# Talking-heads attention with a squared-ReLU FFN: fusing the first twenty query tiles instead of twelve

## The chip, the cores and the metric

The kernel runs on one core of a Trainium2 chip. The metric is the device time of one execution in microseconds (us). Three runs of the kernel before gave 600.27, 600.85 and 602.12 us; the median, 600.85 us, stands for it. Times inside the execution are read from one profiled execution and are counted from its first instruction. The engines are named as the profile names them: PE is the matrix engine (PEld its weight loads), DVE the vector engine, ACT the scalar engine, POOL the GpSimd engine, and SP the engine that here only issues DMAs.

## The reference, cut to what matters

For each of 8 batches there are 12 heads, 448 positions and a head size of 64. The scores of the heads are mixed by a 12x12 matrix before the softmax, and the probabilities by another one after it; the result, put back into rows of 768, goes through an FFN with a squared ReLU.

```python
scores = scale * np.matmul(q, k.transpose(0, 1, 3, 2))
scores = np.einsum('bhij,hg->bgij', scores, w_pre)
scores = scores - np.max(scores, axis=-1, keepdims=True)
attn = np.exp(scores)
attn = attn / (np.sum(attn, axis=-1, keepdims=True) + 1e-09)
attn = np.einsum('bhij,hg->bgij', attn, w_post)
x = np.matmul(attn, v)            # then rows (b, i) of 12*64 = 768
h = np.maximum(x @ w_in, 0.0)     # 768 -> 2048
out = h * h @ w_out               # 2048 -> 768
```

## The kernel before, in words

**Tiles and steps.** A query tile is 10 query rows with all 12 heads: 120 partitions by 448 keys. There are 45 of them in a batch (the last has 8 rows), 360 in all, and one pass of the main loop (L465) is one step: the mix of tile i, the unmix of tile i - 4 (`LAG`), and pieces of other work between them. Step i begins on PE with the tile's `m_ps` matmul, so the steps can be counted in the trace.

**The mix (L369)** brings the mixed scores of a tile into PSUM (`m_ps`); ACT takes the exponential and the row sum (L384), DVE the reciprocal (L386), and POOL scales the second mixing matrix by it (`pn`, L388). **The unmix (L392)** multiplies the exponentials with `pn` in four matmuls (`at_ps`, L401) and DVE copies the result out (L403).

**Two ways to the mixed scores.** The plain way: a block of 128 query rows is scored head by head (`score_burst`, L320: 12 matmuls `s_ps` over 64 rows of the array, in two bursts of six), ACT and DVE copy the 12 results into an SBUF block `S` (L342, L344; there are two such blocks, used in turn), and SP's queue gathers from it, tile by tile, 10 rows of 12 heads into `G` (L361: 120 pieces of 896 bytes, 105 KB). One matmul of `G` with the mixing matrix then gives `m_ps` (L381). The fused way, for the first `FUSED` = 12 tiles of batch 0: DVE multiplies the queries by the mixing weights beforehand (`mix_queries`, L176), and six matmuls over 128 rows give `m_ps` straight from queries and keys (L376). It needs no `S`, no copies and no gather. The multiplied queries are kept in the FFN's second weights `w2[0..2]`, which are not loaded yet.

In batch 0 the plain tiles are 12 to 44. Their three blocks begin at rows 120, 240 and 320; the first and the third use the same `S` buffer, the second and the first block of batch 1 the other. `BURSTS` says at the issue of which gather the bursts of the next block are put: those of batch 0's third block come at steps 19 and 22, those of batch 1's first block at steps 29 and 32.

**What sets the order.** PE's and POOL's order is the order of the program text; on the others a scheduler sets it. Gathers are issued up to 10 tiles ahead (`AHEAD`), from step 2 on. Loads from HBM that change the type are issued by POOL at fixed steps, each in front of the step's other work: keys and queries of batch 1 at steps 5, 7, ... 15 (`KQ_AT`), the first half of the FFN's first weights (three pieces of 512 KB) before and during the first steps, the second half at steps 18, 21 and 24 (`W1_AT`), the second weights in eight pieces from step 30 to 51 (`W2_AT`). Transposes of batch 1's keys and queries run at steps 17, 21 and 25 (`TURN`), the product with v of the first 15 tiles at step 21.

FFN units are the filler. Batch 0's first FFN half is done in thirds of the positions: 16 units of six matmuls (`h_ps`, L251) for each third, of which the first eight use the first half of the first weights and the last eight the second half. `EARLY` says from which step a group may be spread over the steps: the first third's units from steps 21 (first eight) and 32 (last eight), the second third's from 38, the last third's from 52. ACT takes the ReLU (L257, two buffers `hr`), POOL the square (L262).

The loads of each step, the mix, the fill, the unmix, the gathers and the bursts follow one another like this:

```python
            if s0:
                mix(s0)
            for w, f in now:
                f()
                owed[0] -= w
            fill(share)
            if s1:
                unmix(s1)
...
            if i + 1 < end:
                fill(share)
```

## Time and profile before

| what | value |
|---|---|
| three runs | 600.27, 600.85, 602.12 us |
| the profiled execution, its own time | 600.99 us |
| its span, first to last instruction | 599.2 us |
| PE busy | 574.3 us (96%) |
| DVE / ACT / POOL busy | 69% / 64% / 54% |
| mean granted PE clock | 0.995 |
| start of step 0, 12, 20, 23, 50, 60 on PE | 15.03, 34.17, 44.14, 50.77, 82.36, 99.44 us |

The busy shares are means over stages with different limits. A matmul's record reaches from its start to a modelled end, so a stretch in which matmuls follow each other slowly can look full; the starts of the steps say more than the shares. The last row of the table is counted from the timeline of PE: the n-th tile's first `m_ps` matmul is the start of step n.

### The profile page before, as it was taken

The numbers are of one execution on the slowest core, as the hardware profiler recorded it, in microseconds if no ns is written. First come the engines' busy times: TensorE is split into PE (matmuls) and PEld (weight loads), VectorE is DVE, ScalarE is ACT, GpSimd is POOL, SyncE is SP. The second block draws the span as 40 slices with busy tenths as digits, with TensorE's granted clock in tenths as the row PEclk, the third lists the DMA queues.
The fourth block names the chain that finished last, engine by engine and source line by source line (L and its number), as shares of the span: only waits on it lengthen the run. The fifth ranks groups of instructions, "written<-read, shape, count | busy, mean of one in ns | idle before, by whom it ended". The sixth has DMA issues, their size and how long they took to land.

```text
span 599.2 us, 17220 instructions
## 1 busy us (share of the span) xinstructions
PE 574.3 (96%) x6011; PEld 372.2 (62%) x6011; DVE 411.7 (69%) x1044; ACT 380.6 (64%) x1105; POOL 326.1 (54%) x708
## 2 busy tenths in 40 slices
PE   4979999899999999999999999999999999999996
PEld 3547777566566666566565665666665666666553
DVE  5668769988767777767777777777867667666011
ACT  3757978676876557864776547775677547762410
POOL 5354897362777227862569316792377325761730
PEclk9999999999999999999999999999999999999999
DMA  9898999698569755795458855697544755431003
GB/s 128 141 199 164 191 197 196 128 172 193 100 101 140 145 100 109 121 156 124 98 94 135 151 111 101 113 143 138 109 79 69 133 119 107 84 50 54 27 27 79
DMA packets 88279, 72.28 MB, mean 121 GB/s; under 512 B 6688, under 2 KB 83200, under 8 KB 88192
## 3 DMA queue, kind: packets, MB, share of 16 engines
q1 hardware_dynamic: 50394, 48.16, 36.6%
q0 software_dynamic: 37216, 22.81, 29.3%
q8 instruction: 47, 0.77, 0.5%
q10 hardware_dynamic: 582, 0.21, 0.2%
q14 instruction: 40, 0.33, 0.1%
HBM read 45.70 MB, written 11.01 MB: 95 GB/s over the span
## 4 chain that ended last, share of the span: by engine, by line
PE 81%; DMA 10%; ACT 3%; issue 2%; DVE 1%; POOL 1%; SPq 1%; ACTq 0%; POOLq 0%; DVEq 0%
PE o_ps L295 24%; PE h_ps L251 22%; PE at_ps L401 10%; PE m_ps L381 10%; DMA G<-S 7%; PE ot_ps L209 6%; PE s_ps L332 4%; PE tr_ps L193 3%; ACT e L384 2%; DMA w<-in_moe_w_in_dram 2%; DMA kst<-in_k_dram 1%; ACT S L342 1%; PE m_ps L376 1%; DVE S L344 1%; PE s_ps L338 1%
## 5 line engine op out<-in xcount | busy, mean ns | idle before, releaser
L403 DVE CAST at<-at_ps 112x480 bf16<-112x480 f32 x360 | 228.5, 650 | 73.3 <-PE at_ps L401 72.8
L384 ACT ACTIVATE e<-m_ps 120x448 bf16<-120x448 f32 x360 | 195.5, 547 | 98.8 <-PE m_ps L381 92.4
L388 POOL TENSOR_SCALAR pn<-post,rc 120x120 bf16<-120x120 bf16 x348 | 129.0, 372 | 207.1 <-DVE rc L386 147.6
L251 PE MATMUL h_ps<-xt,w 128*128 128x448 bf16 (+2 forms) x960 | 169.6, 315 | 1.1 <-ACT hr L257 0.6
L295 PE MATMUL o_ps<-w,h 128*128 128x384 bf16 x768 | 138.7, 326 | 0.3 <-ACT S L342 0.2
L401 PE MATMUL at_ps<-pn,e 120*128 120x120 bf16 (+1 forms) x1440 | 135.1, 216 | 0.7 <-POOL pn L388 0.5
L401 PEld LDWEIGHTS <-e 120*128 120x128 bf16 (+1 forms) x1440 | 103.9, 98 | 45.0 <-issue 1.4
L381 PE MATMUL m_ps<-G,pre 120*120 120x448 bf16 x348 | 124.6, 358 | 2.1 <-ACT S L342 1.0
L251 PEld LDWEIGHTS <-w 128*128 128x128 bf16 x960 | 84.6, 98 | 57.7 <-issue 5.6
L262 POOL TENSOR_TENSOR h<-hr 128x384 bf16<-128x384 f32 (+1 forms) x144 | 106.1, 738 | 19.4 <-ACT hr L257 15.6
L257 ACT ACTIVATE hr<-h_ps 128x448 f32<-128x448 f32 (+2 forms) x160 | 75.4, 473 | 52.7 <-PE h_ps L251 35.9
L295 PEld LDWEIGHTS <-h 128*128 128x128 bf16 x768 | 72.8, 98 | 48.2 <-issue 5.5
L344 DVE CAST S<-s_ps 128x448 bf16<-128x448 f32 x159 | 89.2, 615 | 4.2 <-DMA G<-S 2.3
L386 DVE RECIPROCAL rc<-sm 120x1 f32<-120x1 f32 x360 | 57.2, 159 | 45.2 <-ACT e L384 37.3
L342 ACT CAST S<-s_ps 128x448 bf16<-128x448 f32 x171 | 79.8, 546 | 11.9 <-PE s_ps L332 8.4
L384 ACT ACTIVATION_READ_ACCUMULATOR e<-m_ps 120x1 f32 x360 | 74.1, 206 | 0.0
L304 DVE COPY osb<-o_ps 128x384 f32<-128x384 f32 x54 | 30.1, 557 | 46.8 <-PE o_ps L295 46.6
L381 PEld LDWEIGHTS <-pre 120*120 120x120 bf16 x348 | 46.1, 133 | 20.9 <-issue 14.6
L332 PE MATMUL s_ps<-kT,qT 64*128 64x448 bf16 x288 | 41.5, 355 | 5.8 <-ACT S L342 4.4
L209 PE MATMUL ot_ps<-at,v 112*64 112x150 bf16 x1152 | 42.6, 230 | 0.0
L209 PEld LDWEIGHTS <-v 112*64 112x64 bf16 x1152 | 38.3, 110 | 4.9 <-issue 4.9
L215 ACT CAST xt<-ot_ps 128x450 bf16<-128x450 f32 (+1 forms) x48 | 25.5, 533 | 20.4 <-PE ot_ps L209 19.9
(45 smaller groups left out, 288.2 us busy)
## 6 DMA issues: line engine op xcount, KB each, us to landing
G<-S SPq DMA_DIRECT2D x284, 105.0 KB
qst<-in_q_dram POOLq DMA_DIRECT2D x24, 224.0 KB, 5.7
kst<-in_k_dram POOLq DMA_DIRECT2D x24, 224.0 KB, 5.2
v<-in_v_dram POOLq DMA_DIRECT2D x24, 224.0 KB, 6.9
G<-S SPq DMA_DIRECT2D x70, 52.5 KB
w<-in_moe_w_in_dram POOLq DMA_DIRECT2D x6, 512.0 KB, 10.3
w<-in_moe_w_out_dram POOLq DMA_DIRECT2D x8, 384.0 KB, 7.7
out_dram<-osb SPq DMA_DIRECT2D x8, 336.0 KB
```

What stands on the lines that cost most here:

```text
L209: nc.tensor.matmul(ps[64 * hh:64 * hh + 64, TQ * y:TQ * y + TQ], lhsT=vs[b][0:PR, g, r, :], rhs=at[0:PR, r, g, :], start=(y == 0 and r == ...
L251: nc.tensor.matmul(ps[:, 0:n], lhsT=w1[ft // 8][:, c2, ft % 8 * 128:ft % 8 * 128 + 128], rhs=xts[b][:, c2, n0:n1], start=(c2 == 0), stop=( ...
L257: nc.scalar.activation(out=hr[:, 0:n], in_=ps[:, 0:n], func=ACT.Relu)
L262: eng.tensor_tensor(out=dst[:, x - o:y - o], in0=hr[:, x - n0:y - n0], in1=hr[:, x - n0:y - n0], op=ALU.mult)
L295: nc.tensor.matmul(ps[:, 0:384], lhsT=lhsT, rhs=w2[ft // 4][:, ft % 4, nt * 384:(nt + 1) * 384], start=(ft == 0), stop=(ft == FT - 1))
L342: nc.scalar.copy(out=sb[:, h, :], in_=ps[:, 0:S])
L344: nc.vector.tensor_copy(out=sb[:, h, :], in_=ps[:, 0:S])
L381: nc.tensor.matmul(ps[0:n, 0:S], lhsT=m[0:n, 0:n], rhs=Gs.pop(s)[0:n, :], start=True, stop=True)
L384: nc.scalar.activation(out=e[0:n, 0:S], in_=ps[0:n, 0:S], func=ACT.Exp, scale=SCALE, accum_out=sm[0:n, 0:1])
L388: nc.gpsimd.tensor_scalar(out=pn[0:n, :], in0=(post_gi if fused else post)[0:n, :], scalar1=rc[0:n, 0:1], scalar2=1.0, op0=ALU.mult, op1=A ...
L401: nc.tensor.matmul(ps[:, RG * r:RG * r + RG], lhsT=e[0:n, PR * r:PR * r + P], rhs=pn[0:n, :], start=True, stop=True)
L403: nc.vector.tensor_copy(out=ats[(b, third)][0:PR, :, :, IQ * tl:IQ * tl + IQ], in_=ps[0:PR, 0:R * RG].rearrange("p (r g i) -> p r g i", r= ...
```

## The change

`FUSED` becomes 20: tiles 0 to 19 of batch 0 are fused. The multiplied queries of the first 12 (`SOON`) stay in `w2[0..2]`; those of tiles 12 to 19 go to three other buffers that are not in use yet (`w2[3]`, the second `v` buffer and one of the two `xt` buffers), and their six multiplications are placed at steps 3, 4 and 5. The remaining 25 tiles of batch 0 come from two blocks, at rows 200 and 320, with first tiles 20 and 32; each has an `S` buffer to itself. The bursts of the second block come at steps 4 and 6, those of batch 1's first block, which uses the first block's buffer again, at steps 27 and 30. Keys and queries of batch 1 are loaded one step sooner; the second half of the first weights is loaded at steps 15, 17 and 19, not 18, 21 and 24, and the units that use it may begin at step 28, not 32. The function `fused_part` holds the six matmuls; it is called only by `mix`, so their place in the order is the old one.

```diff
--- before.py
+++ after.py
@@ -22,12 +22,13 @@
 IQ = 10
 NT = 45
 RG = H * IQ
-FUSED = 12
+FUSED = 20
+SOON = 12
 FQ = FUSED * IQ
 NEAR = 4
-STARTS = {0: (FQ, 2 * FQ, S - 128)}
-FIRST = {0: (FUSED, 2 * FUSED, 3 * FUSED)}
-BURSTS = {0: ([5, 8], [5, 8], [3, 6])}
+STARTS = {0: (FQ, S - 128)}
+FIRST = {0: (FUSED, 32)}
+BURSTS = {0: ([4, 8], [5, 8])}
 for _b in range(1, B):
     STARTS[_b], FIRST[_b], BURSTS[_b] = (0, 128, 256, 384), (0, 13, 26, 39), ([5, 8], [5, 8], [6], [0, 3])
 GATHERS_AT = 2
@@ -38,11 +39,11 @@
 AHEAD = 10
 SCALE = 1.0 / 8.0
 TURN = {0: (17, 17, 21, 21, 25, 25), 1: (20, 20, 24, 24, 28, 28), B: (1 + LAG,) * 3 + (16 + LAG,) * 3}
-KQ_AT = {1: (5, 7, 9, 11, 13, 15), 2: (52, 54, 56, 58, 60, 62)}
-W1_AT = (-1, 1, 3, 18, 21, 24)
+KQ_AT = {1: (4, 6, 8, 10, 12, 14), 2: (52, 54, 56, 58, 60, 62)}
+W1_AT = (-1, 1, 3, 15, 17, 19)
 W2_AT = (30, 33, 36, 39, 42, 45, 48, 51)
 V1_AT = (47, 50, 53)
-EARLY = ((21, 0, 0, 2), (32, 0, 2, 4), (38, 1, 0, 4), (52, 2, 0, 4))
+EARLY = ((21, 0, 0, 2), (28, 0, 2, 4), (38, 1, 0, 4), (52, 2, 0, 4))
 FFN2_AT = 60
 MAIN = 3 * 128
 
@@ -166,14 +167,21 @@
 
     qTs, kTs, xts, h2ts, ats = {}, {}, {}, {}, {}
 
-    qmix = [w2[u][:, :, :].rearrange("p c m -> p (c m)")[:, 0:2 * FQ * H].rearrange(
-        "p (y t g i) -> p y t g i", y=2, g=H, i=IQ) for u in range(NPAIR // 2)]
+    late = [w2[3][:, :, :].rearrange("p c m -> p (c m)"), stage_tile("v", 2)[:, :, :, :].rearrange("p h r d -> p (h r d)"),
+            ffnp.tile([P, NPAIR, S], BF16, name="xt", tag="xt", bufs=2)[:, :, :].rearrange("p c s -> p (c s)")]
+
+    def mixed(u, y, t0, t1):
+        if t0 < SOON:
+            buf, x = w2[u][:, :, :].rearrange("p c m -> p (c m)"), SOON * y + t0
+        else:
+            buf, x = late[u], (FUSED - SOON) * y + t0 - SOON
+        return buf[:, RG * x:RG * (x + t1 - t0)]
 
     def mix_queries(u, t0, t1):
 
         for y in range(2):
             qs = qTs[0][:, 2 * u + y, IQ * t0:IQ * t1].rearrange("p (t i) -> p t i", i=IQ)
-            nc.vector.tensor_tensor(out=qmix[u][:, y, t0:t1, :, :],
+            nc.vector.tensor_tensor(out=mixed(u, y, t0, t1).rearrange("p (t g i) -> p t g i", g=H, i=IQ),
                                     in0=qs.unsqueeze(2).to_broadcast([P, t1 - t0, H, IQ]),
                                     in1=wrep[:, 2 * u + y, :, :].unsqueeze(1).to_broadcast([P, t1 - t0, H, IQ]),
                                     op=ALU.mult)
@@ -352,7 +360,7 @@
         g = work.tile([P, S], BF16, name="G", tag="G", bufs=AHEAD + 2)
         x, end = IQ * t, min(IQ * t + IQ, S)
         while x < end:
-            blk = x // P if b else min(x // FQ, 3) - 1
+            blk = max(y for y, q0 in enumerate(STARTS[b]) if q0 <= x)
             n = min(end, STARTS[b][blk] + P) - x
             o, y = H * (x - IQ * t), x - STARTS[b][blk]
             sb = Sb[(b, blk)]
@@ -366,17 +374,29 @@
             x += n
         Gs[s] = g
 
+    parts = {}
+
+    def fused_part(t, u):
+
+        if t not in parts:
+            parts[t] = [0, bank("m_ps")]
+        if parts[t][0] > u:
+            return
+        parts[t][0] = u + 1
+        for p in (2 * u, 2 * u + 1):
+            nc.tensor.matmul(parts[t][1][0:RG, 0:S], rhs=kTs[0][:, p, :], lhsT=mixed(u, p % 2, t, t + 1),
+                             start=(p == 0), stop=(p == NPAIR - 1))
+
     def mix(s):
         n = rows_of(s[1])
         b, t = s
-        ps = bank("m_ps")
         fused = b == 0 and t < FUSED
         if fused:
-            for p in range(NPAIR):
-                nc.tensor.matmul(ps[0:n, 0:S], rhs=kTs[b][:, p, :],
-                                 lhsT=qmix[p // 2][:, p % 2, t, :, :].rearrange("p g i -> p (g i)"),
-                                 start=(p == 0), stop=(p == NPAIR - 1))
+            for u in range(NPAIR // 2):
+                fused_part(t, u)
+            ps = parts[t][1]
         else:
+            ps = bank("m_ps")
             m = pres[max(x for x in pres if x <= t)] if b else pre
             nc.tensor.matmul(ps[0:n, 0:S], lhsT=m[0:n, 0:n], rhs=Gs.pop(s)[0:n, :], start=True, stop=True)
         e = ets[(NT * s[0] + s[1]) % ND]
@@ -428,7 +448,7 @@
         for u in range(NPAIR // 2):
             turn_unit(0, 0, u)
             mix_queries(u, 0, NEAR)
-            mix_queries(u, NEAR, FUSED)
+            mix_queries(u, NEAR, SOON)
             turn_unit(0, 1, u, nc.scalar.copy)
             if u == 1:
                 score_burst(0, 0, [0, 1])
@@ -497,10 +517,12 @@
                         at_step(i + 3, u)
                 if t1 == NT - 1:
                     at_step(i + 3 if b1 else FFN2_AT, (0, lambda b1=b1: filler.extend(ffn_units(b1))))
+            if 2 < i < 6:
+                mix_queries(i - 3, SOON, FUSED)
             if i < 2:
                 score_burst(0, 0, [2 + 2 * i, 3 + 2 * i])
             for _ in range(2 if i >= GATHERS_AT else 0):
-                if ahead[0] > min(max(i + AHEAD, 2 * FUSED - 1), len(steps) - 1):
+                if ahead[0] > min(max(i + AHEAD, FIRST[0][1] - 1), len(steps) - 1):
                     break
                 b2, t2 = steps[ahead[0]]
                 gather((b2, t2))
```

## The prediction

> **What bounds the kernel now.** I read the page's busy shares and its chain first, then PE's timeline step by step, then the waits.

> ```profile
> PE 574.3 (96%) x6011; PEld 372.2 (62%) x6011; DVE 411.7 (69%) x1044; ACT 380.6 (64%) x1105; POOL 326.1 (54%) x708
> PE 81%; DMA 10%; ACT 3%; issue 2%; DVE 1%; POOL 1%; SPq 1%; ACTq 0%; POOLq 0%; DVEq 0%
> ```

> PE is the bound, but a tenth of the chain is DMA: a part of the run is not PE's. All the change's edits lie in steps 0 to 49. From step 50 on the two programs have the same instructions in the same order on every engine, so the question is when step 50 begins (82.36 us before). In PE's timeline:

> ```profile
> 31.26 0.38 PE L401 MATMUL at_ps<-pn,e 120*128 120x120 bf16 x4
> 31.47 1.30 PE L376 MATMUL m_ps<-kT,w 128*120 128x448 bf16 x6
> 32.61 0.38 PE L401 MATMUL at_ps<-pn,e 120*128 120x120 bf16 x4
> 32.82 1.30 PE L376 MATMUL m_ps<-kT,w 128*120 128x448 bf16 x6
> ...
> 38.66 0.35 PE L381 MATMUL m_ps<-G,pre 120*120 120x448 bf16 x1
> 38.97 0.37 PE L401 MATMUL at_ps<-pn,e 120*128 120x120 bf16 x4
> 39.27 0.96 PE L332 MATMUL s_ps<-kT,qT 64*128 64x448 bf16 x5
> 43.71 0.35 PE L332 MATMUL s_ps<-kT,qT 64*128 64x448 bf16 x1 [3.47 <-ACT S L342]
> 44.14 0.53 PE L381 MATMUL m_ps<-G,pre 120*120 120x448 bf16 x1
> ```

> A fused step takes 1.35 us from start to start (32.82 less 31.47), and PE runs through it; a plain step takes 0.40 us. After step 19 PE puts the third block's first burst and stands still. ACT says why:

> ```profile
> 39.61 0.20 ACT L384 ACTIVATION_READ_ACCUMULATOR e<-m_ps 120x1 f32 x1
> 43.12 1.84 ACT L342 CAST S<-s_ps 128x448 bf16<-128x448 f32 x4 [3.31 <-DMA G<-S]
> ```

> The third block's copies go into the `S` buffer that the gathers of tiles 12 to 23 are still reading; ACT waits for the last of these, and PE for the PSUM banks that ACT doesn't empty. The bill continues:

> ```profile
> core 0: us, PE busy (x) PEld busy (x) DVE busy (x) ACT busy (x) POOL busy (x), PEclk, DMA share, GB/s
> 34.17:44.14 9.97, 6.16 (x82) 3.73 (x79) 7.56 (x22) 5.95 (x21) 6.18 (x14) 1.00 1.14 202
> 44.14:50.77 6.63, 6.60 (x105) 5.21 (x105) 4.07 (x12) 4.15 (x12) 1.52 (x4) 0.74 0.94 191
> 50.77:82.36 31.59, 29.93 (x413) 23.75 (x414) 25.98 (x67) 27.81 (x96) 24.53 (x58) 1.00 0.91 178
> 82.36:99.44 17.08, 16.12 (x227) 12.95 (x225) 13.80 (x52) 13.72 (x49) 14.93 (x28) 1.00 1.15 204
> ```

> These are steps 12-19, 20-22, 23-49 and 50-59. Right after the stall the granted clock averages 0.74 (it is 0.5 for 3.4 us), and PE looks busy at half speed.

> **The change, part by part.**

> *Steps 12 to 19* (before 9.97 us). Each becomes a fused step: 8 x 1.35 = 10.8. The 32 transposes of step 17 stay: that step took 1.74 against 0.40, and 1.41 where nothing else hindered it (steps 65 and 69), so about 1.0. Stall and burst of step 19 go: the third block no longer exists, and the two blocks have a buffer each. Sum 11.8: **+1.8 us**. So the stall alone doesn't pay for the fused matmuls; filling it costs a little more than it. ACT needs about 0.75 (0.55 + 0.20) and DVE 0.81 (0.66 + 0.15) a step, under 1.35, so PE sets this pace.

> *Steps 20 to 22* (before 6.63). The second burst goes: step 22 took 1.51, a plain one 0.40, so -1.1. At full clock step 20 takes 0.40 (before 0.72) and step 21 3.25 (before 4.40): 0.40 for the tile, 1.0 for the transposes, 1.7 for `ot_ps` (66.41 to 68.10 later on), 0.16 for `pre_ps`. Sum 4.05: **-2.6 us**, of which 1.5 are the clock's.

> The row shows only that half clock follows the stall. [...]

> *Multiplying queries* (steps 3-5). The rows of this shape in DVE's timeline give 1.87 us for two of 480 and two of 960 elements, so some 0.62 for a 960: six are 3.7 us of DVE. In the new instruction lists the scheduler puts one ahead of each of the last two early groups, and four among the first copies of `S`. DVE idled 0.22 and 0.40 us ahead of those groups; the first `m_ps` needs the last group only for its fifth matmul, 1.4 us after its first. The reciprocals of tiles 1 to 3 come up to 1 us later, with 4 steps of 1.35 us before PE asks. Between 0 and 0.9 (two multiplications fully exposed less what idled); I take **+0.15**, near the covered end, since every row around it has slack.

> *Steps 23 to 49* (before 31.59). PE has the same work in both programs: 27 mixes and unmixes, the same 29 FFN units, the same bursts of batch 1, only at other steps (eight units now run in steps 26 and 27). Priced back to back by the timeline's own rows (six `h_ps` 0.39, a tile 0.40, `s_ps` 0.095 each, 48 `ot_ps` 1.75, 32 transposes 0.65 in the stream), before needed 26.75 and lost 4.84. Of that 1.9 recurs whatever the order (transposes 0.36, bursts 0.3 each, small gaps 0.3). The other 2.9 are pockets: step 29 lost 1.13 (a burst whose copies met the ReLUs on ACT), step 32 0.71, step 33 0.42 (it waits for the first weights), steps 48-49 0.60 (POOL late), step 28 0.38. After: no wait for the first weights if they land in time, the bursts at steps 27 and 30 carry two units fewer around them in sum, one FFN unit fewer falls into steps 38-49; against that stands the bunch of eight units at 26-27, which POOL squares at some 0.42 us each, about as fast as PE makes them. Ends: -2.9 (all pockets go) to +1.0 (bunch and weights cost more than what goes). I take half of the pockets, **-1.4**, since two of five have a named reason to go.

> *Second half of the first weights.* The old landing and the new need:

> ```profile
> 53.41 9.94 DMA w<-in_moe_w_in_dram
> ```

> That wait was on the chain: PE stood at step 33. Now the last piece is issued behind step 18's `pn`, at about 46, and the DMAs of this queue took 7.8 to 11.5 us from issue to landing between 24 and 54: so 53.8 to 57.5. PE reaches step 29, the first user, at 34.17 + 0.15 + 11.8 + 4.05 + (23 to 28: 7.6 to 8.0) = about 57.8 to 58.2. Cost nothing, with little to spare; what a late landing costs is a rival below. Nothing is exchanged on POOL but the order: three issues of 0.75 us move from steps 18-24 to 15-19, where POOL has 1 us free per step. The gathers shrink by eight; tiles 20-31 are issued from step 2 on as tiles 12-23 were, landing by 43, ahead of step 20 at 46.

> *From step 50*: the same order, nothing to gain; loads and gathers are issued by steps and move along. PE waits about 3 us at steps 72-74 for batch 2's last queries and keys, which land at 111.9 and 114.4 behind a full queue; -0.5 to +0.7.

> Sum: 0.15 + 1.8 - 2.6 - 1.4 = **-2.0 us**. The profiled execution took 600.99 us, 0.02% off the median of 600.85; against the median this is **598.8 us**.

> **The rivals.**

> *The pockets stay.* PE's work is net +7 us, and the stall returns as small waits on ACT and POOL in steps 23-49: the -1.4 becomes 0 to +0.7, the sum -0.6 to +0.1, near **600.5**. For: POOL and ACT are 78% and 88% busy there. Against: ACT and DVE lose 12 copies of some 0.5 us that lay in steps 19-24.

> *Slower: PE waits for the first weights at step 29.* For: in the first half a piece issued 3.3 us after the one before landed 8.2 us after it (24.5 and 32.7). If the keys and queries land at 47.9 (before 47.7), the first two pieces at their old spacing (51.2, 54.7) and the third 8.2 later, that is 62.9: PE waits 5.1 us, and since that exceeds the 3.47 of the old stall, half clock costs 1.5 more: -2.0 + 6.6, **605.4**. It eats the gain from a landing at 59.8 on. [...] Against: none of the nine landings around it took over 11.5 us, and this one would take 17.

> *All pockets go*: -2.9 in their place and nothing exposed on DVE, **597.2**. That the change doesn't do what it says is ruled out by the instruction lists: 40 `m_ps` more, 12 `s_ps`, 12 copies and 8 gathers fewer.

> **How the numbers follow.** A time within 0.3% (1.8 us) is about what a measurement of this kernel can't tell from no change. Forecast (1 to 2.9 us gained) 0.50, pockets stay 0.27, all pockets go 0.13, weights late 0.10. The forecast's case lies with 0.35 beyond 1.8 us and 0.15 within; of the staying pockets 0.02 is faster, 0.24 the same, 0.01 slower. So faster 0.35 + 0.13 + 0.02 = 0.50, same 0.15 + 0.24 = 0.39, slower 0.10 + 0.01 = 0.11. The low end is the third rival with the 0.5 of step 50 on top, 596.6. At the high end DVE at +0.9 in place of +0.15 and the pockets at +1.0 in place of -1.4 make 602.0; with +0.7 at step 73 as well it would be 602.7, but all three ends at once are rarer than what may be left out, as are the late weights.

> **What would show it.** No wait over 1 us of PE on `S` between 34 and 50 us, and the granted clock at 1.00 there (right); step 12 at 34.2 to 34.5; step 20 at 46.1; step 23 at 50.2; step 50 at 80.4. A step 20 later than 47, or a wait on `in_moe_w_in` at step 29, breaks the sum; a step 23 as told but step 50 at 82 means that the pockets stayed. If step 50 comes sooner and the end doesn't, the loads at steps 72-74 took it back.

## The result, and the profile after

Over 17 runs of each the changed kernel took a median of 602.9 us and the kernel before 600.86 us: a ratio of **1.0031, with a 95% interval of 1.0017 to 1.0045**. The change makes the kernel slower by about 2 us, where 2 us of gain were forecast. The profiled execution took 604.16 us, 1.3 us more than the median, so the differences in its trace end somewhat larger than 2 us; its span is 602.0 us (before 599.2). The page's busy shares and chain:

```profile
PE 580.9 (96%) x6039; PEld 376.0 (62%) x6039; DVE 412.8 (69%) x1046; ACT 377.9 (63%) x1097; POOL 327.1 (54%) x708
PE 88%; DMA 5%; ACT 3%; issue 1%; POOL 1%; DVE 1%; ACTq 0%; POOLq 0%; DVEq 0%
```

DMA's part of the chain has halved, from 10% to 5%. By the page alone one would think that the change did its work. Where the time went is told by the starts of the steps on PE (the tile's first `m_ps`), side by side:

| step | before, us | after, us | after less before |
|---|---|---|---|
| 12 | 34.17 | 34.51 | +0.34 |
| 20 | 44.14 | 46.32 | +2.18 |
| 23 | 50.77 | 50.27 | -0.50 |
| 28 | 54.05 | 58.06 | +4.01 |
| 50 | 82.36 | 80.89 | -1.47 |
| 60 | 99.44 | 97.98 | -1.46 |
| 74 | 115.14 | 114.47 | -0.68 |
| 75 | 117.40 | 117.62 | +0.22 |
| 79 | 123.06 | 125.82 | +2.76 |

From step 79 on the difference stays between +2.75 and +2.88 to the end. So the early steps gained the 1.5 us, and 4.2 us were lost after step 60, in steps whose instructions are the same in both kernels.

The first steps scatter from trace to trace: in the other nine traces with twenty fused tiles, which come below, step 12 begins at 33.29 to 34.88 us. A difference of 1.5 us at one step of one trace is therefore worth little by itself. Counted from step 12 it is clear: step 50 comes 48.19 us later in the kernel before, 46.38 us later in the changed one, and 46.33 to 46.35 in the three other traces that share its tables (`e1`, `e8`, `e12`).

The early part first, in PE's timeline and in the stretches of the kernel before (columns as before: busy time and instructions of PE, PEld, DVE, ACT, POOL; granted clock; DMA share; GB/s):

```profile
46.10 0.38 PE L421 MATMUL at_ps<-pn,e 120*128 120x120 bf16 x4
46.32 0.35 PE L401 MATMUL m_ps<-G,pre 120*120 120x448 bf16 x1
```

```profile
34.17:44.14 9.97, 9.97 (x101) 7.25 (x100) 5.17 (x15) 4.45 (x14) 5.86 (x12) 1.00 1.12 179
44.14:50.77 6.63, 6.63 (x123) 5.40 (x120) 5.03 (x14) 3.90 (x12) 2.19 (x5) 1.00 1.03 180
50.77:82.36 31.59, 30.30 (x421) 23.84 (x419) 26.02 (x70) 27.04 (x97) 25.18 (x60) 1.00 0.83 165
```

The wait of 3.47 us on `S` is gone, PE is busy in all of the first two rows, and the clock is 1.00 in the second, where it was 0.74. Now the place of the loss, PE's timeline in steps 73 to 75 of the changed kernel (the end of a line is the idle time before it and what ended it):

```profile
112.00 0.58 PE L201 MATMUL tr_ps<-ident,kst 112*64 112x112 bf16 x16
113.73 0.58 PE L201 MATMUL tr_ps<-ident,qst 112*64 112x112 bf16 x16 [1.15 <-DMA qst<-in_q_dram]
...
115.54 0.37 PE L340 MATMUL s_ps<-kT,qT 64*128 64x448 bf16 x2 [0.22 <-ACT e L404]
117.13 0.56 PE L340 MATMUL s_ps<-kT,qT 64*128 64x448 bf16 x2 [1.22 <-ACT S L350]
117.62 0.63 PE L401 MATMUL m_ps<-G,pre 120*120 120x448 bf16 x1
```

The same wait on the last queries, and the two lines on the burst, in the kernel before:

```profile
114.41 0.58 PE L193 MATMUL tr_ps<-ident,qst 112*64 112x112 bf16 x16 [1.12 <-DMA qst<-in_q_dram]
...
116.97 0.36 PE L332 MATMUL s_ps<-kT,qT 64*128 64x448 bf16 x2 [0.39 <-ACT S L342]
117.40 0.35 PE L381 MATMUL m_ps<-G,pre 120*120 120x448 bf16 x1
```

Two things differ. PE reaches the burst sooner and waits 1.22 us for the copies into `S` instead of 0.39. And the durations after it are longer: an `s_ps` pair 0.56 against 0.36, an `m_ps` 0.63 against 0.35. The granted clock is at 0.5 from 116.4 us on, for 6.8 us. ACT's line shows what its copies wait for, in the changed kernel and then in the kernel before:

```profile
116.55 0.97 ACT L350 CAST S<-s_ps 128x448 bf16<-128x448 f32 x2 [1.06 <-DMA G<-S]
```

```profile
116.39 1.50 ACT L342 CAST S<-s_ps 128x448 bf16<-128x448 f32 x3 [0.22 <-DMA G<-S]
```

In both kernels the copies go on at about 116.5 us, when the gathers that read the old block have landed. PE came 0.7 us sooner; the gathers did not. The 4.22 us between step 60 (-1.46) and step 79 (+2.76) divide so: 0.78 given back up to step 74, 0.90 in step 74 (the wait above), and 2.54 in steps 75 to 78, which took 8.20 us (125.82 less 117.62) against 5.66: the half clock. The 0.78 is not all the queues': 0.41 is step 64, which takes 2.10 or 2.11 us in every other trace of this case and 1.70 only in the kernel before, and 0.35 are steps 69 and 71, which take as much longer in all ten traces with twenty fused tiles. But it doesn't matter to this kernel where they went: the last load of queries landed only 0.67 us sooner than before (113.69 for 114.36), and PE waited for it, so step 74 could not have come much sooner than it did.

### The profile page after: what moved, and what is told of

The parts are those of the page before. It is cut to its first block, busy times and chain, and to the rows that moved or that the text cites. A ratio compares the mean times of both kernels' runs of the same rounds, so it can differ in the third digit from the quotient of the medians.

```text
span 602.0 us, 17243 instructions
## 1 busy us (share of the span) xinstructions
PE 580.9 (96%) x6039; PEld 376.0 (62%) x6039; DVE 412.8 (69%) x1046; ACT 377.9 (63%) x1097; POOL 327.1 (54%) x708
## 4 chain that ended last, share of the span: by engine, by line
PE 88%; DMA 5%; ACT 3%; issue 1%; POOL 1%; DVE 1%; ACTq 0%; POOLq 0%; DVEq 0%
PE o_ps L303 25%; PE h_ps L259 23%; PE at_ps L421 12%; PE m_ps L401 11%; PE ot_ps L217 6%; PE s_ps L340 4%; PE m_ps L387 4%; PE tr_ps L201 3%; DMA qst<-in_q_dram 2%; DMA G<-S 1%; DMA kst<-in_k_dram 1%; ACT e L404 1%; ACT S L350 1%; PE s_ps L346 1%; POOL h L270 1%
## 5 line engine op out<-in xcount | busy, mean ns | idle before, releaser
L408 POOL TENSOR_SCALAR pn<-post,rc 120x120 bf16<-120x120 bf16 (+1 forms) x340 | 127.0, 375 | 203.3 <-DVE rc L406 143.1
L303 PE MATMUL o_ps<-w,h 128*128 128x384 bf16 x768 | 140.4, 328 | 0.1
L401 PE MATMUL m_ps<-G,pre 120*120 120x448 bf16 (+1 forms) x340 | 122.3, 360 | 2.0 <-ACT S L350 1.2
L303 PEld LDWEIGHTS <-h 128*128 128x128 bf16 x768 | 73.4, 98 | 49.3 <-issue 7.3
L352 DVE CAST S<-s_ps 128x448 bf16<-128x448 f32 x155 | 86.8, 614 | 1.2 <-DMA G<-S 0.9
L350 ACT CAST S<-s_ps 128x448 bf16<-128x448 f32 x163 | 76.3, 547 | 9.6 <-PE s_ps L340 8.6
L401 PEld LDWEIGHTS <-pre 120*120 120x120 bf16 (+1 forms) x340 | 45.2, 133 | 17.9 <-issue 10.9
L340 PE MATMUL s_ps<-kT,qT 64*128 64x448 bf16 x276 | 39.9, 357 | 2.8 <-ACT S L350 1.2
```

The source lines that it names most:

```text
L303: nc.tensor.matmul(ps[:, 0:384], lhsT=lhsT, rhs=w2[ft // 4][:, ft % 4, nt * 384:(nt + 1) * 384], start=(ft == 0), stop=(ft == FT - 1))
L350: nc.scalar.copy(out=sb[:, h, :], in_=ps[:, 0:S])
L352: nc.vector.tensor_copy(out=sb[:, h, :], in_=ps[:, 0:S])
L401: nc.tensor.matmul(ps[0:n, 0:S], lhsT=m[0:n, 0:n], rhs=Gs.pop(s)[0:n, :], start=True, stop=True)
L408: nc.gpsimd.tensor_scalar(out=pn[0:n, :], in0=(post_gi if fused else post)[0:n, :], scalar1=rc[0:n, 0:1], scalar2=1.0, op0=ALU.mult, op1=A ...
```

## The experiments

The theory from these traces: the queues did not move along with PE, and the waits at their end left PE so little to do that the clock was halved. Rivals: the matmuls of steps 75 to 78 are slowed by something else (a DMA, a full PSUM); the loss comes from the fused matmuls themselves and not from the tables of loads and units. Ratios are to the kernel before, on the same chip.

**Is it the clock, and do the waits cause it?** `e1_busy` is the changed kernel with useless matmuls behind the last transposes of the keys and in the burst of step 74, twelve in all; `e8_thin` is its control, the same matmuls with 16 columns (`0:16`) in place of 448.

```diff
+        if (b, which, u) == (2, 0, 2):
+            spare = bank("spare_ps")
+            for x in range(6):
+                nc.tensor.matmul(spare[:, 0:S], lhsT=ident[:, :], rhs=kTs[1][:, x, :], start=(x == 0), stop=(x == 5))
```

(The same four lines stand in `score_burst` for `(b, blk, p) == (2, 0, 2)`.)

> The changed kernel with 12 useless matmuls of 448 columns on PE, six in step 73 where PE waits for the last queries of batch 2, six in step 74 in front of the last pair of the burst, where it waits for the copies of S. Nothing reads them. Gate theory (the loss at steps 74 to 78 is half clock, which falls because PE does too little in the waits): the granted clock stays at 1.00 from 108 to 124 us, step 79 comes at about 123.1 in place of 125.8, time about 600.2 (2.7 under the changed kernel's 602.9), though PE has 2.3 us more to do. Queue theory (the loads and gathers set the pace there, clock or not): step 79 stays at 125 or later, time 602.5 to 605.

> A control for e1: the same 12 useless matmuls, but of 16 columns each, so that the order, the PSUM bank and the weight loads are e1's and PE gets 0.3 us of work in place of 2.3. Gate theory: half clock falls near 116 us as in the changed kernel, time 602 to 603. If e1 gained by another way (the extra bank, the order), this gains too: 600 to 601.

Measured: `e1_busy` 600.49 us, ratio 0.9996 (0.9982 to 1.001); `e8_thin` 603.9 us, 1.002 (1.0 to 1.004). The two traces, PE in `e1_busy`, then the stretch 118 to 123 us in `e1_busy` and 113 to 118 us in `e8_thin`:

```profile
112.61 1.31 PE L198 MATMUL spare_ps<-kT,ident 128*128 128x448 bf16 x6
...
115.94 1.29 PE L343 MATMUL spare_ps<-kT,ident 128*128 128x448 bf16 x6
...
117.61 0.40 PE L409 MATMUL m_ps<-G,pre 120*120 120x448 bf16 x1
```

```profile
118.00:123.00 5.00, 5.00 (x44) 2.98 (x42) 3.67 (x9) 2.88 (x10) 1.83 (x4) 1.00 0.69 114
```

```profile
113.00:118.00 5.00, 4.38 (x39) 2.41 (x40) 4.53 (x11) 2.05 (x5) 1.83 (x4) 0.52 0.37 71
```

With 2.6 us of useless work in the holes (1.31 and 1.29), step 75 begins at 117.61 as in the changed kernel (117.62), the clock stays at 1.00, and step 79 begins at 122.77: 3.05 us sooner. With the same number of instructions, but 16 columns wide, the clock falls to half at 113.2 for 6.8 us. The two ran on two chips, but the fall goes with the width in nearly all their runs: the mean clock is 0.998 or more in 11 of the 12 of `e1` and in 1 of the 12 of `e8`. Only the width differs between the two, so the granted clock (1.00 and 0.52 in the stretches above) makes the loss of steps 75 to 78, and too little work for PE makes the clock fall here. But `e1_busy` only breaks even with the kernel before: the other 1.7 us (0.78 and 0.90) were lost ahead of the fall, up to the wait in step 74.

```profile
112.44:115.86 3.42, 2.30 (x47) 1.57 (x45) 3.42 (x11) 1.31 (x5) 1.47 (x4) 1.00 0.47 119
```

```profile
113.03:116.45 3.42, 1.96 (x29) 1.17 (x30) 3.42 (x11) 0.63 (x2) 1.33 (x5) 1.00 0.39 97
```

| kernel, start of the window | PE busy of 3.4 us | clock after it |
|---|---|---|
| before, 40.76 | 0.39 | half |
| `e11`, 70.55 | 1.19 | half |
| `e7`, 55.49 | 1.45 | half |
| changed 113.03; `e12` 113.59 | 1.96; 1.96 | half |
| `e8`, 109.81 | 2.01 | half |
| `e4` 114.61; `e10` 69.43 | 2.17; 2.24 | full |
| `e2`, 111.32 | 2.27 | half |
| before, 112.44 | 2.30 | full |
| `e9` 111.90; `e6` 111.94; `e1` 113.10 | 2.47; 2.63; 3.19 | full |

In these windows the clock fell after every one with up to 2.01 us and after none from 2.30 us on; in between it held at 2.17 and 2.24 and fell at 2.27 (a row of PE can reach 0.17 us over the start of the next, as 57.29 and 0.94 over 58.06 below, so a tenth is not to be trusted). The other windows of the fourteen traces agree: the falls that the table leaves out, in `e3` and `e4`, come after 0.49 to 1.86 us, and no window that kept the clock has less than the 2.17 of `e4`. The kernel before stood just on the good side: it had the same holes, and 0.34 us more work in its window. It doesn't stand there in every run: of its 90 runs beside the experiments 28 have a mean clock of 0.991 or less, and their median is 602.9 us, against 601.0 for the other 62 (no profile of these is kept). The window ahead of the fall was not idle: the changed kernel's was 57% busy (1.96 of 3.42), and no single wait around it was longer than 1.22 us. The grid lies differently from trace to trace (the window starts at 113.03 and at 113.59 us in the two of the changed kernel), which may be why its runs differ: of 23 runs of the changed kernel (these 17 and the six of `e12`), two had a mean clock of 0.998 or more, at 600.77 and 601.32 us; the median of the other 21 is 603.19 us.

How long the clock stays down can be read in the same way, from the window after the fall. In the changed kernel it stayed at half for a second window, in `e2` it did not:

```profile
116.45:119.86 3.41, 2.69 (x9) 1.02 (x9) 2.07 (x5) 2.13 (x5) 1.32 (x3) 0.50 0.65 79
```

```profile
114.73:118.15 3.42, 3.37 (x13) 1.49 (x12) 2.27 (x6) 1.35 (x4) 1.46 (x3) 0.50 0.55 64
```

Of the sixteen windows at half clock between the first full clock and 590 us in the fourteen traces, the five with up to 3.27 us of work at half speed were followed by another at half, and the eleven with 3.33 us or more by full clock. Ahead of the first full clock 3.20 and 3.22 us were enough in two traces (`e8`, `e5`) and 3.21 was not in two others (the changed kernel, `e12`), so this limit isn't sharp either; nothing was run to try it.

**Which part of the change puts the queues behind?** `e9_units_from_32` is the changed kernel with one number put back, so that the eight FFN units that run in steps 26 and 27 are again spread from later on; `e6_fuse_only` puts back all three old tables and keeps the fusing alone; `e4_loads_only` is the kernel before with the three new tables; `e12_change_again` is the changed kernel on the chip of `e9`.

```diff
# e9
-EARLY = ((21, 0, 0, 2), (28, 0, 2, 4), (38, 1, 0, 4), (52, 2, 0, 4))
+EARLY = ((21, 0, 0, 2), (32, 0, 2, 4), (38, 1, 0, 4), (52, 2, 0, 4))
# e6: that line, and (in KQ_AT, batch 1 alone)
-KQ_AT = {1: (4, 6, 8, 10, 12, 14), ...
-W1_AT = (-1, 1, 3, 15, 17, 19)
+KQ_AT = {1: (5, 7, 9, 11, 13, 15), ...
+W1_AT = (-1, 1, 3, 18, 21, 24)
# e4: the lines of e6 the other way round, in the kernel before
```

> The changed kernel with the three tables of the kernel before (keys and queries at steps 5 to 15, second half of the first weights at 18, 21 and 24, its units from step 32): only the twenty fused tiles and the two blocks. From my sum for the steps, step 23 comes 0.4 to 0.5 us sooner than in the kernel before, as in the changed kernel, and step 50 0.5 to 1.5 us sooner. If the loss at steps 74 to 78 is of the queues and the gate, it shows here too: 601.5 to 603.5. If the loss came with the moved tables, this is below 600.3.

> The changed kernel with one number taken back: the last eight units of the first third may begin at step 32, as before, not 28, so that the first eight are no longer bunched in steps 26 and 27. Bunch theory (the units in 26 and 27 hold up the gathers and loads that steps 28 to 33 issue by up to 3.7 us, and the queues never make it good before step 74): like the run with the fused tiles alone, step 28 at about 54.4, step 74 below 113.6, no half clock near 115, ratio to the kernel before about 0.996. If the earlier weight loads are what hurts: like the changed kernel, 1.003.

> The kernel before with only the change's three tables of times: keys and queries of batch 1 one step sooner, second half of the first weights at steps 15, 17, 19, its units from step 28. If the gain by step 50 (1.47 us) is the fused tiles' and the stall's, this shows at most 0.5 us of it (the 0.42 of waiting at step 33), with the stall at 39 to 44 and the half clock unchanged or worse, since more loads run against the gathers: 600 to 602. If the gain is the loads', step 50 comes 1.2 to 1.5 us sooner than before.

> The changed kernel once more, beside the others on their chip. Gate theory: runs with a mean clock of 0.998 and more are near 600.5 to 601.5, those at 0.992 to 0.996 near 602.5 to 604.5; ratio to the kernel before 1.000 to 1.004, and above e9's by 0.4 to 0.7%.

| kernel | median, us | ratio (95%) | step 50 | step 79, each less before |
|---|---|---|---|---|
| `e6_fuse_only` | 600.1 | 0.9962 (0.9944 to 0.9981) | -1.43 | -1.39 |
| `e9_units_from_32` | 599.91 | 0.999 (0.9972 to 1.0008) | -1.60 | -0.95 |
| `e12_change_again` | 603.63 | 1.0051 (1.0031 to 1.0071) | -1.20 | +3.36 |
| `e4_loads_only` | 602.75 | 1.0024 (1.0007 to 1.0041) | +1.14 | +1.94 |

One number decides between `e9` and `e12`, on one chip: 3.7 us of median, and every run of `e12` is slower than every run of `e9`. Both have the early gain; only `e9` keeps most of it. Its ratio, 0.999, is not the 0.996 that was expected of it; the distance to `e12` is. PE in `e9` in steps 73 to 75:

```profile
113.01 0.58 PE L201 MATMUL tr_ps<-ident,qst 112*64 112x112 bf16 x16 [0.60 <-DMA qst<-in_q_dram]
...
116.02 0.36 PE L340 MATMUL s_ps<-kT,qT 64*128 64x448 bf16 x2 [0.83 <-ACT S L350]
```

Both waits are shorter (0.60 and 0.83 for 1.15 and 1.22), and its thinnest windows have 2.46 and 2.47 us of work, so the clock holds. How the number may reach step 73 is seen at its own place, in the changed kernel:

```profile
55.74 1.50 PE L340 MATMUL s_ps<-kT,qT 64*128 64x448 bf16 x6
57.29 0.94 PE L259 MATMUL h_ps<-xt,w 128*128 128x150 bf16 x12
58.06 0.35 PE L401 MATMUL m_ps<-G,pre 120*120 120x448 bf16 x1
```

The last units of the bunch and a burst of batch 1 stand ahead of step 28, which begins at 58.06 us and in `e9` at 54.22. Loads and gathers are issued by steps, and the first gathers after that go out up to 2.9 us later than in `e9`. PE has caught up by step 50. One reading is that the DMAs have not: in the page's line of DMA digits the three slices from 60 to 105 us are 9 tenths or more (in both kernels), and with no room a late start would stay late. The traces bear this out only in part. From step 50 on `e6` issues its loads at the same times as the changed kernel (the last at 101.73 us in both); its last one lands at 112.52, the changed kernel's at 113.69 us, but those issued from 80.5 to 87.7 us land 0.5 to 1.2 us later in `e6` than in the changed kernel. The chain of the changed kernel shows that load:

```profile
101.73 11.96 DMA qst<-in_q_dram
```

Before, it was issued at 102.98 and landed at 114.36 us: issued 1.25 us sooner, it lands 0.67 sooner. That the difference between `e9` and `e12` is made by this number is shown; that it goes by way of the delayed issues is a guess, not tried by itself. `e6` met the expectation for the tables as the cause, not the one for the fusing. `e4` has none of the gain and keeps the stall at step 19, so the gain up to step 50 is the fusing's and not the loads'. Ratios from different chips compare less well than `e9` and `e12` do: the median of the kernel before is 601.27 us beside `e4`, 602.28 beside `e6` and 601.00 beside `e9`, while `e6` and `e9` themselves are 0.2 us apart.

**Can the queues be given room?** `e2_w2_sooner` is the changed kernel with the eight pieces of the second weights issued nine or more steps sooner; `e5_w2_sooner_busy` has the useless matmuls of `e1` as well. `e10` and `e11` are the same two with the number of `e9`. `e3_before_w2_sooner` does it to the kernel before, with (26, 28, 30, 32, 34, 36, 38, 40).

```diff
-W2_AT = (30, 33, 36, 39, 42, 45, 48, 51)
+W2_AT = (21, 23, 25, 28, 31, 34, 37, 40)
```

> The changed kernel with the eight pieces of the second weights loaded at steps 21 to 40, not 30 to 51, so that the last keys and queries of batch 2 find an emptier queue. Both theories: the wait at step 73 (1.7 us and what follows) shrinks if the queue was the cause of it. Gate theory: with the wait goes the half clock, step 79 at about 119 to 120, time 597 to 598. Queue theory without a gate: the 1.5 us gained by step 60 and some 2 us of waits, 599 to 600. If the waits at steps 72 to 74 stay as they are: 602 to 603.

> Both edits of e1 and e2 on the changed kernel: second weights at steps 21 to 40, and the 12 useless matmuls of 448 columns in steps 73 and 74. Gate theory: no half clock between 20 and 590 us, step 79 about 1.5 us sooner than e2's 121.9, time 597 to 598. Queue theory: the same as e2, 598.8, or worse by the 2.3 us of useless work.

> The kernel before with the second weights loaded at steps 26 to 40, not 30 to 51. If the queue at steps 72 to 74 costs both kernels alike, this gains the 3 us that it stands there: 597.5 to 598.5, and the old stall and half clock at 39 to 48 us stay. Then the change by itself is worth e2 less e3, about -1.5 us as at step 50. If the queue theory is wrong and the waits are of another cause, it stays at 600.5 to 601.

> As e9, with the second weights at steps 21 to 40 as well. If what is left at steps 73 to 77 is the queues', another 1 to 1.5 us sooner than e9, ratio 0.993 to 0.995. If the earlier loads push gathers back instead (as in the kernel before with them, 1.012), slower than e9.

> As e10, with the 12 useless matmuls of 448 columns in steps 73 and 74. If half clock still falls there in some runs of e10, this is steadier and 0 to 1.5 us faster than e10; if PE no longer waits there, the useless work costs up to 2.3 us.

| kernel | median, us | ratio (95%) |
|---|---|---|
| `e2_w2_sooner` | 598.83 | 0.998 (0.9953 to 1.0007) |
| `e5_w2_sooner_busy` | 599.66 | 0.9965 (0.9945 to 0.9986) |
| `e3_before_w2_sooner` | 607.77 | 1.0117 (1.0098 to 1.0136) |
| `e10_units32_w2_sooner` | 603.21 | 1.0044 (1.0021 to 1.0068) |
| `e11_units32_w2_busy` | 602.69 | 1.0046 (1.0023 to 1.007) |

In `e2` step 60 came 2.82 us sooner than before and step 74 3.38, but then PE waited 1.11 us on `S` and the clock fell for 3.4 us, which left -1.15 at step 79; with the useless matmuls (`e5`) there is no fall, and -2.97 stays (0.6 of it from an earlier step 20). The fall is not the rule in `e2`: eight of its twelve runs have a mean clock of 0.999 or more. The other three were slower than the kernel before. `e3` went against its expectation; `e10` met the second of its two, slower than `e9`; `e11` is within noise of `e10` and decides nothing. The chain and PE's timeline of `e3` say how:

```profile
60.58 15.31 DMA G<-S
```

```profile
77.08 0.53 PE L381 MATMUL m_ps<-G,pre 120*120 120x448 bf16 x1 [4.17 <-ACT S L342]
```

The weights brought forward fell on the gathers of steps 30 to 45: one took 15.31 us in the chain from issue to landing (the longest in the chain of the kernel before, up to 100 us, took 9.95), the copies into `S` waited for it, PE for these, and the clock halved for 6.8 us at 75.2. In `e10` the same wait was 2.13 us at 73.80; its trace is of a run without a fall (601.41 us, clock 0.999), and nine of its twelve runs have a lower mean clock. What tells `e2`, which gained, from `e10`, which lost, is the steps at which units, loads and gathers meet; I have not taken it further apart.

**The old half clock alone.** `e7_before_busy` is the kernel before with 18 useless matmuls (as in `e1`, over `kTs[0][:, x % 6, :]`) in `score_burst` at `(b, blk, p) == (0, 2, 2)`, the stall of step 19.

> The kernel before with 18 useless matmuls of 448 columns on PE in front of the last pair of the burst at step 19, where PE stands for 3.5 us. Gate theory: the granted clock stays at 1.00 from 17 us on, at least to 110 us; the stall stays, but step 23 comes 1.3 to 1.5 us sooner than in the kernel before (49.3), and the time falls to 599.4 if nothing behind takes it back. If half clock there is due to anything else than PE's idleness, it stays at 0.74 for steps 20 to 22 and the time is 600.9 or more.

Measured 602.87 us, ratio 1.0012 (0.9987 to 1.0036). The clock stays at 1.00 at 44 us, and steps 20 to 22 took 5.09 us, not 6.63: 1.54 us went with the half clock, where the prediction put 1.5. But they did not reach the end: at 57.81 us PE waits 1.96 us for a copy into `S`, which waits 1.79 us for a gather, the clock halves at 58.9, and at the end the kernel is 1.4 us behind. It is the same story at an earlier block: PE sooner, the queue not.

## Why the prediction was wrong, point by point

- *DVE's six multiplications* (+0.15): +0.34 at step 12, inside the bounds given; step 12 began at 33.29 to 34.88 us in the other traces with twenty fused tiles, so no more can be said.
- *Steps 12 to 19* (+1.8): 11.81 us (46.32 less 34.51) against 9.97, so +1.84. Right.
- *Steps 20 to 22* (-2.6): 3.95 us against 6.63, so -2.68; full clock and no wait on `S` between 34 and 50 us. Right, and `e7` shows by itself that the half clock there follows the stall. That the 1.5 us of clock in the -2.6 go with the stall no run had shown when it was forecast; in `e7`, with the stall filled, 1.54 us went.
- *Steps 23 to 49* (-1.4): 30.62 us against 31.59, so -0.97. Between "half of the pockets go" and "they stay"; the bunch at steps 26 and 27 made a new pocket of some 1.1 us at step 27. Step 50 began at 80.89, forecast 80.4. The sum up to there, -2.0, measured -1.47: a term mis-sized by 0.4, and the sign right. The five pockets that the prediction names add up to 3.24 us, not 2.9; less the 0.3 that recurs in each of the two bursts among them it is 2.64.
- *Second half of the first weights*: the last piece landed at 55.13 us, step 29 began at 58.50 and waited for none. The rival of late weights did not happen, and its price stayed untested.
- *"From step 50: the same order, nothing to gain; loads and gathers are issued by steps and move along"*, -0.5 to +0.7: **this step failed.** It measured +4.2 between step 60 and step 79: 2.54 of half clock, 0.90 of waiting for `S` in step 74, 0.78 ahead of it. The loads were issued sooner, but up to 12.6 us passed between issue and landing in this stretch, and the last landed 0.67 us sooner where it was issued 1.25 sooner; the copies of step 74 could go on 0.16 us later than before. The prediction had this backlog in view ("land at 111.9 and 114.4 behind a full queue") and still let it move along. It also put PE's wait there at about 3 us, where PE was idle for 2.0 us of steps 72 to 74 (3.79 us busy of 5.81). With the old number in `EARLY` the step holds: between step 60 and step 79 it is +0.06 in `e6` and +0.68 in `e9`. So what the prediction missed is that the bunch at steps 26 and 27, priced inside steps 23 to 49 alone, has its cost after step 60. By which way it gets there stays open.
- *The clock*: the prediction priced a half clock only for a wait longer than the old 3.47 us, at step 29. Here waits of 1.15 and 1.22 us were enough, as parts of both and smaller gaps fell into one window, 1.46 us in sum. `e1` against `e8` shows it, with 2.5 us. Without that fall the changed kernel would have been even with the kernel before, not faster: at step 75 it was already 0.22 us behind, and `e1`, without the fall, 0.21.
- *"If step 50 comes sooner and the end doesn't, the loads at steps 72-74 took it back"*: so it came, in place, though the loads alone did not take it back: the wait for the last queries is 1.15 us for 1.12, and the rest is the wait for `S` and the clock. The place was named as a sign, not priced as a rival, and that is why no case of the prediction but the late weights, which did not happen, reaches 602.9.

Fusing alone does what the sum said up to step 50 and keeps it: `e6_fuse_only`, 0.9962, is the only version without useless work whose interval lies wholly below 1; `e5` has the same with useless work, and `e2` (0.998) can't be told from either. The tables that came with the fusing undid it, above all the one number that lets the last eight units begin at step 28.

## What to carry to other kernels

A stretch that waits for DMAs need not move along when the work ahead of it gets shorter (here the last load was issued 1.25 us sooner and landed 0.67 sooner): for a change early in a program, follow each load and gather of the next full stretch from issue to landing before carrying a gain to the end. Where PE arrived early it waited, and short waits close together cost more than their own time: those of 1.15 and 1.22 us, with smaller gaps, left 1.96 us of work in a window of 3.42, and the half clock after it cost 2.54 us on top. A step made heavier delayed the transfers that the next steps issue (here by up to 2.9 us), even though PE caught up.

## What the runs showed that I had not expected

- The clock fell after a window in which PE was 57% busy; filling the holes with 2.6 us of useless matmuls made the kernel faster (600.49 us, against a changed kernel of 602.9 and a control of 603.9, each on other chips; their ratios are 0.9996, 1.0031 and 1.002).
- Bringing 8 pieces of 384 KB forward by four to eleven steps cost the kernel before 1.2% (`e3`), through gathers between two places of SBUF, one of which took 15.31 us.
- Once fallen, the clock stayed at half for 3.4 us in some traces and 6.8 in others, also where the window after the fall was 77 to 96% busy by the records (`e12`, `e8`, `e4`). It came back after windows that PE filled almost wholly, with 3.33 us or more of 3.41.
